# Sparse attention and a feed-forward block on one core: weight sums in halves, 2 KB store pieces, fewer zero products and a new table of steps

## The chip, the cores and the metric

The kernel runs on one core of a Trainium2 chip. The metric is the device time of one execution in microseconds, by the median of several runs. The core's engines are TensorE (PE; PEld is its weight load), VectorE (DVE), ScalarE (ACT), GpSimd (POOL) and SyncE (SP). DMAs are issued by SyncE and, for the stores of weights, by ScalarE.

## What is computed

Eight batches of attention with eight heads, 576 positions and 64 dimensions feed a feed-forward block over all 4608 tokens. Four heads see a local window of 32 positions, four see the positions of their own class modulo 32.

```python
scores = scale * np.matmul(q, k.transpose(0, 1, 3, 2))
mask_local = (rel >= 0) & (rel < stride)                      # heads 0 to 3, stride 32
mask_strided = (rel >= 0) & (pos[None, :] % stride == pos[:, None] % stride)   # heads 4 to 7
attn = np.exp(scores - scores.max(-1, keepdims=True))         # masked scores
attn = attn / (attn.sum(-1, keepdims=True) + 1e-09)
x = np.matmul(attn, v).transpose(0, 2, 1, 3).reshape(B * S, H * D)   # 4608 x 512
h = x @ w_in                                                  # 512 x 2048
g = np.where(h >= 1, h, np.where(h <= -1, 0.0, (h + 1) ** 2 / 4))
return g @ w_out                                              # 2048 x 512
```

## The kernel before

A product of float32 matrices is made of three products of 128x512 on TensorE: each operand is split into a rounded high part and a remainder. The 4608 tokens go in nine chunks of 512. The first three chunks are made directly: up(c, f) multiplies chunk c with the f-th of 16 hidden blocks, the gate g follows on ScalarE and VectorE, and for chunk 0 `down` adds the block's share of the output. The other tokens are four groups (s = 0 to 3) made by a Strassen scheme with seven products where the direct one has eight. For s = 0 only the second half of it, `down_block`, is needed; s = 1 to 3 have an `up_block` ahead of it.

The scheme needs sums of blocks of the weights. They are made once, while chunks 1 and 2 run. For pair (i, j), `whole_blocks` adds two parts of the weights (step C on GpSimd, Y on VectorE), `combine` adds on (N on GpSimd, O on VectorE), `round_sums` (R) and `rest_of_sums` (D) split the result, and `ship_sums` (S) stores it to DRAM as ks; `ship` (K) stores plain weights as kq. Later `fetch_w` loads them on SyncE's queue, 256 KB at a time, into a ring of seven buffers wr. Load n + 7 is issued when TensorE is done with n.

Attention goes in units u = 0 to 3 of each batch b (tiles named with `_b_u`). Its steps are: load qk (Q), scores on TensorE (s, tile sc), mask (m), maximum and subtraction (x, a or b, tiles pr and st), exponential (e), sum (q), reciprocal and normalisation (p, k, w, r; VectorE or GpSimd), transpose (t), a store to DRAM and a gather back as pT (j, J, on SyncE), load v (F), and value products on TensorE (v, tile xp) with copies to the next chunks' x (h, l).

All these side steps stand in AGENDA, a table of numbers. A row begins with a time t in units of six 128x512 products (1.36 us); t = 0 is up(1, 0), t = 68 the start of the first down block. A step is put into every engine's program when the loop over products comes to its time, so the table alone sets the order on each engine and in SyncE's queue. A step with zeros (`zero`) issues products of zeros in the first batch, which keep TensorE going while it has no operands.

Of the kernel before, what the change touches and what calls it, by code (L numbers as in the profile page):

```python
# [1326 lines left out]
```

## Time and profile before

| | |
|---|---|
| median of three runs | 806.49 us (804.26 to 806.54) |
| the profiled execution | 806.21 us, its span 804.4 us |
| TensorE busy | 793.8 us, 99% of the span |
| VectorE busy | 620.6 us, 77% |
| ScalarE busy | 505.2 us, 63% |
| GpSimd busy | 258.2 us, 32% |
| DMA | 209.78 MB, 261 GB/s in the mean |

All times of rows are in us from the start of the span of that one execution. A row's line number (L499) is the line of the kernel before; the changed kernel's lines are 7 or 8 higher.

### The profile page before, as it was taken

Reading aid. Unit: us, or ns where it says so; the run is one execution under the profiler, and the core shown is the slowest. Engines: PE = TensorE matmul, PEld = TensorE weight load, DVE = VectorE, ACT = ScalarE, POOL = GpSimd, SP = SyncE. Lnnn points to the kernel's source line nnn. Section 1 sums busy time; section 2 is a strip of 40 time slices with the busy share of each in tenths; the row PEclk is TensorE's granted clock in tenths of the full one; section 3 lists DMA queues with packets and bytes.
Section 4 is the critical chain, followed back from the end, with each engine's and each line's share of the span. In section 5 each row is a group of like instructions: output and inputs, shape, how many; then the busy total and the mean of one; then the engine's idle time right before and its main releaser. Section 6 shows DMA issues by size and latency. Waiting matters only on the chain.

```text
span 804.4 us, 17840 instructions
## 1 busy us (share of the span) xinstructions
PE 793.8 (99%) x6921; PEld 648.5 (81%) x6921; DVE 620.6 (77%) x882; ACT 505.2 (63%) x857; POOL 258.2 (32%) x202
## 2 busy tenths in 40 slices
PE   8999999999999999999999999999999999999998
PEld 6778888788888877878888888888888888888886
DVE  5899879999898999978679787575777764566673
ACT  5899764566774555677764455778554667775442
POOL 5366335796674320022141102132434001224000
PEclk9999999999999999999999999999999999999999
DMA  9948878799899899898889778777777676666765
GB/s 348 407 187 273 319 271 324 254 290 307 282 322 319 292 295 352 272 295 275 256 247 292 239 222 266 261 233 211 223 248 239 210 238 198 192 194 189 217 200 170
DMA packets 107699, 209.78 MB, mean 261 GB/s; under 512 B 17760, under 2 KB 33376, under 8 KB 105568
## 3 DMA queue, kind: packets, MB, share of 16 engines
q1 hardware_dynamic: 100560, 179.15, 69.8%
q10 hardware_dynamic: 7056, 29.49, 9.5%
q8 instruction: 55, 0.90, 0.4%
q14 instruction: 28, 0.23, 0.1%
HBM read 161.94 MB, written 46.66 MB: 259 GB/s over the span
## 4 chain that ended last, share of the span: by engine, by line
PE 91%; DVE 5%; ACT 1%; DMA 1%; issue 1%; POOL 1%; SPq 0%; POOLq 0%; DVEq 0%
PE yo L1135 22%; PE y L1040 16%; PE h L887 13%; PE zo L1135 10%; PE z L1040 8%; PE xo L1135 5%; PE o L947 4%; PE x L1040 4%; PE xp L779 3%; PE sc L592 3%; DMA qk<-in_qk_s 1%; PE tp L719 1%; DVE st L512 1%; DVE pr L682 1%; DVE st L678 0%
## 5 line engine op out<-in xcount | busy, mean ns | idle before, releaser
L1135 PE MATMUL yo<-hl,wr 128*128 128x512 f32 x768 | 177.6, 390 | 0.0
L1135 PEld LDWEIGHTS yo<-hl,wr 128*128 128x128 f32 x768 | 143.6, 188 | 30.9 <-DVE hl L997 0.9
L1040 PE MATMUL y<-x,wr 128*128 128x512 f32 x576 | 139.9, 389 | 0.0
L1040 PEld LDWEIGHTS y<-x,wr 128*128 128x128 f32 x576 | 108.0, 188 | 22.5
L887 PE MATMUL h<-xq_a,w 128*128 128x512 f32 x384 | 123.5, 395 | 1.9 <-DVE g L897 1.9
L1096 POOL TENSOR_TENSOR ga<-gb,ga 128x1024 f32<-128x1024 f32 x17 | 44.1, 2598 | 235.9 <-DVE ga L897 175.6
L997 DVE TENSOR_TENSOR hl<-ga,hl 128x1024 fp32r<-128x1024 f32 x48 | 63.5, 1338 | 37.0 <-ACT hl L996 36.9
L1135 PE MATMUL zo<-hl,wr 128*128 128x512 f32 x384 | 89.5, 391 | 0.0
L887 PEld LDWEIGHTS h<-xq_a,w 128*128 128x128 f32 x384 | 72.0, 188 | 18.6 <-DVE g L897 2.8
L1135 PEld LDWEIGHTS zo<-hl,wr 128*128 128x128 f32 x384 | 71.5, 188 | 15.9 <-DVE hl L997 0.6
L996 ACT CAST hl<-ga 128x1024 fp32r<-128x1024 f32 x48 | 50.0, 1052 | 51.1 <-PE yo L1135 16.3
L887 PE MATMUL h<-xq_b,w 128*128 128x512 f32 x192 | 73.6, 391 | 0.1
L1040 PE MATMUL z<-x,wr 128*128 128x512 f32 x288 | 73.5, 391 | 0.0
L1040 PEld LDWEIGHTS z<-x,wr 128*128 128x128 f32 x288 | 53.7, 188 | 11.4 <-DVE ga L1022 0.2
L894 ACT ACTIVATE tmp<-tmp 128x512 f32<-128x512 f32 x96 | 60.8, 634 | 3.0
L997 DVE TENSOR_TENSOR hl<-gb,hl 128x1024 fp32r<-128x1024 f32 x36 | 48.7, 1366 | 14.4 <-ACT hl L996 14.3
L996 ACT CAST hl<-gb 128x1024 fp32r<-128x1024 f32 x36 | 37.7, 1056 | 31.3 <-PE zo L1135 15.3
L504 POOL TENSOR_TENSOR st<-st 128x256 f32<-128x256 f32 x48 | 50.5, 1054 | 14.2 <-DVE st L705 6.6
L897 DVE SCALAR_TENSOR_TENSOR ga<-ga,tmp 128x512 f32<-128x512 f32 x48 | 33.0, 688 | 28.3 <-ACT tmp L894 28.0
L891 ACT ACTIVATE u<-h,half 128x512 f32<-128x512 f32 x48 | 32.8, 684 | 31.4 <-PE h L887 23.9
L469 POOL TENSOR_TENSOR raw<-raw 128x512 uint32<-128x512 uint32 (+1 forms) x34 | 35.6, 1057 | 42.3 <-DVE raw L465 16.6
L682 POOL TENSOR_TENSOR pr<-pr,st 128x384 f32<-128x384 f32 (+3 forms) x17 | 25.6, 1508 | 67.8 <-DVE st L678 67.8
(124 smaller groups left out, 1413.1 us busy)
## 6 DMA issues: line engine op xcount, KB each, us to landing
wr<-ks SPq DMA_DIRECT2D x224, 256.0 KB, 4.0
wr<-kq SPq DMA_DIRECT2D x168, 256.0 KB, 3.4
ks<-st ACTq DMA_DIRECT2D x16, 1024.0 KB, 6.8
raw<-in_w SPq DMA_DIRECT2D x30, 512.0 KB, 9.6
qk<-in_qk_s SPq DMA_DIRECT2D x16, 604.0 KB, 6.4
qk<-in_qk_l SPq DMA_DIRECT2D x16, 576.0 KB, 6.4
kq<-w ACTq DMA_DIRECT2D x16, 512.0 KB, 3.6
v<-in_v_l SPq DMA_DIRECT2D x21, 384.0 KB, 5.2
```

Of the source, the lines that this page charges most:

```text
L469: nc.gpsimd.tensor_tensor(out=raw[:, :, 1], in0=raw[:, :, 1], in1=raw[:, :, 0], op=ALU.add)
L504: eng.tensor_tensor(out=st[:, to, 1], in0=st[:, x, 1], in1=st[:, y, 1], op=op)
L682: eng.tensor_tensor(out=pr, in0=pr, in1=st[:, 0].unsqueeze(2).broadcast_to(list(pr.shape)), op=ALU.add)
L887: nc.tensor.matmul(o_ps[c, f], weight(f, 0, h)[:, x, e:e + P], xq[c][y][:, cc], start=first and n == 0, stop=last and n == len(todo) - 1)
L891: nc.scalar.activation(u, h, AF.Relu, bias=half, scale=0.5)
L894: nc.scalar.activation(u, u, AF.Square)
L897: nc.vector.scalar_tensor_tensor(out=to, in0=h, scalar=1.0, in1=u, op0=ALU.max, op1=ALU.min)
L996: nc.scalar.copy(t[:, 0], src)
L997: nc.vector.tensor_tensor(out=t[:, 1], in0=src, in1=t[:, 0].bitcast(F32), op=ALU.subtract)
L1040: nc.tensor.matmul(to, w_[:, a, c * P:(c + 1) * P], xc[m][:, b, c], start=m in (1, 2, 5) and c + q == 0, stop=c == 1 and q == 2, skip_grou ...
L1096: eng.tensor_tensor(out=to, in0=x, in1=y, op=op)
L1135: nc.tensor.matmul(to, w_[jj][:, a, d * P:(d + 1) * P], t[:, b, jj], start=m in (1, 2, 5) and k + jj + q == 0, stop=k == NP // 2 - 1 and j ...
```

## The change

A weight sum on GpSimd becomes two instructions of 128x512 where it was one of 128x1024; on VectorE it stays one. The DRAM tiles of weights and sums get the block index in front, so that a store writes pieces of 2 KB (kq 4 and 2 KB, ks 8 KB before) and a ring load reads one run of 256 KB. The products of zeros are as wide as their tile, up to 384 columns, and 24 where they were 37. AGENDA is new behind batch 0 (for batch 0 only the counts of zeros change), and MORE, the set of products that use two further PSUM banks, goes with it. Of the table the diff shows the rows that place batch 5's first qk loads (5Q0) and its unit 1 (5s1).

```diff
 AGENDA = """
--66.69 0Zs0:17 0o0 0s0 0o1 0i0 0X0 0s1 0i1 0S0 0o3 0g1 0x1 0s2 0Zv0:3 0Zf0:3 0m2 0e0 0a1 A0.0 0s3 0i3 0e1 0x2 0q0
+-66.69 0Zs0:10 0o0 0s0 0o1 0i0 0X0 0s1 0i1 0S0 0o3 0g1 0x1 0s2 0Zv0:2 0Zf0:2 0m2 0e0 0a1 A0.0 0s3 0i3 0e1 0x2 0q0
...
-69 G0p33 5Q0
...
-103 G0s52 5Q2 O07 G0s53 5s1 D06 5m1 R07 D07 5x1 5a1
...
+71 4e3 G0s13 R05 G0t60 D05 5Q0 G0s20
...
+77 4t2 4j2 5s1 5m1 5x1
...
+97 5Q2 G0s73 5m0 5x0 Y07
...
-    kept = [[(dram.tile([P, 3, 2, HF], F32, tag=f"kq{i}{j}", name=f"kq_{i}_{j}"),
-              dram.tile([P, 4, 2, HF], F32, tag=f"ks{i}{j}", name=f"ks_{i}_{j}")) for j in range(NP)] for i in range(2)]
+    kept = [[(dram.tile([3, P, 2, HF], F32, tag=f"kq{i}{j}", name=f"kq_{i}_{j}"),
+              dram.tile([4, P, 2, HF], F32, tag=f"ks{i}{j}", name=f"ks_{i}_{j}")) for j in range(NP)] for i in range(2)]
...
-        nc.scalar.dma_start(kept[i][j][0][:, :2], t[:, :2])
-        nc.scalar.dma_start(kept[i][j][0][:, 2], t[:, 3])
+        nc.scalar.dma_start(kept[i][j][0][:2].rearrange("a p x e -> p a x e"), t[:, :2])
+        nc.scalar.dma_start(kept[i][j][0][2], t[:, 3])
...
-        eng.tensor_tensor(out=st[:, :, 1], in0=t[:, :, 0], in1=t[:, :, 1], op=ALU.add)
+        for at in (slice(0, 2), slice(2, 4)) if eng is nc.gpsimd else (slice(0, 4),):
+            eng.tensor_tensor(out=st[:, at, 1], in0=t[:, at, 0], in1=t[:, at, 1], op=ALU.add)
...
-        nc.scalar.dma_start(kept[i][j][1], sums.pop((i, j)))
+        nc.scalar.dma_start(kept[i][j][1].rearrange("a p x e -> p a x e"), sums.pop((i, j)))
...
-            N = min(t.shape[1], 256)
+            N = t.shape[1]
...
-            nc.sync.dma_start(ring[n].bitcast(F32), kept[i][j][which][:, at])
+            nc.sync.dma_start(ring[n].bitcast(F32), kept[i][j][which][at])
...
-    MORE = set("2s2 2v0 2v1 3s0 3s2 3v1 4s0 4s1 4v0 5s0 5s2 5v1 5v2 6s3 7s0 7s1 7v0 7v1".split())
+    MORE = set("2s2 2v0 2v1 3s1 3s2 3v0 4s0 4s2 4v0 4v1 5s0 5s2 5v1 5v2 6s3 7s0 7s1 7s2 7v0 7v2".split())
```

On VectorE, in the stage of up(1, f), after the second transpose of batch 2's unit 1, the order before is this (pr_2_3 and pr_2_2 are units 3 and 2 of batch 2, g_1_0 the gate's result, st_1_3 a weight sum):

```order
L743 STREAM_TRANSPOSE t_2_1_1_2112<-pr_2_1_2039 128x3x2x32
L678 TENSOR_REDUCE st_2_3_2102<-pr_2_3_2101 128x10
L682 TENSOR_TENSOR pr_2_3_2101<-pr_2_3_2101,st_2_3_2102 128x10x54
L652 TENSOR_TENSOR pr_2_2_2135<-sc_2_2_0_2073,m_str_95 128x6x54
L652 TENSOR_TENSOR pr_2_2_2135<-sc_2_2_1_2074,m_str_95 128x6x54
L897 SCALAR_TENSOR_TENSOR g_1_0_1979<-h_1_2_2021,u_1_2_2117 128x512
L678 TENSOR_REDUCE st_2_2_2136<-pr_2_2_2135 128x12
L693 TENSOR_REDUCE st_2_3_2102<-pr_2_3_2101 128x10
```

and now, from the same transpose on:

```order
L751 STREAM_TRANSPOSE t_2_1_1_2073<-pr_2_1_1940 128x3x2x32
L660 TENSOR_TENSOR pr_2_3_2100<-sc_2_3_0_2078,m_str_95 128x4x54
L660 TENSOR_TENSOR pr_2_3_2100<-sc_2_3_1_2079,m_str_95 128x4x54
L660 TENSOR_TENSOR pr_2_3_2100<-sc_2_3_0_2078,m_str_95 64x2x54
L660 TENSOR_TENSOR pr_2_3_2100<-sc_2_3_1_2079,m_str_95 64x2x54
L905 SCALAR_TENSOR_TENSOR g_1_0_1974<-h_1_2_2021,u_1_2_2112 128x512
L686 TENSOR_REDUCE st_2_3_2101<-pr_2_3_2100 128x10
L690 TENSOR_TENSOR pr_2_3_2100<-pr_2_3_2100,st_2_3_2101 128x10x54
L660 TENSOR_TENSOR pr_2_2_2138<-sc_2_2_0_2042,m_str_95 128x6x54
L660 TENSOR_TENSOR pr_2_2_2138<-sc_2_2_1_2043,m_str_95 128x6x54
L507 TENSOR_TENSOR st_1_3_2143<-w_1_3_1067 128x4x256
L686 TENSOR_REDUCE st_2_2_2139<-pr_2_2_2138 128x12
```

The gate of h_1_2 (line L897, now L905) has moved ahead of the reduction and the subtraction (L678 and L682, now L686 and L690) of unit 3 and the masks of unit 2. The subtraction of unit 2, which GpSimd had, is on VectorE now, and so is the sum of block (1, 3).

In SyncE's queue, early in the ring loads for the first down block, batch 5's first two qk loads stand before behind ring load 8:

```order
L971 DMA wr_6_3565<-kq_1_6_181 128x512
L971 DMA wr_7_3581<-kq_1_7_183 128x512
L971 DMA wr_8_3583<-kq_1_0_169 128x512
L525 DMA qk_5_0_3586<-in_qk_l 128x1152
L525 DMA qk_5_1_3588<-in_qk_l 128x1152
L971 DMA wr_9_3602<-kq_1_1_171 128x512
L971 DMA wr_10_3604<-kq_1_2_173 128x512
```

and now behind ring load 10:

```order
L979 DMA wr_6_3557<-kq_1_6_181 128x512
L979 DMA wr_7_3573<-kq_1_7_183 128x512
L979 DMA wr_8_3575<-kq_1_0_169 128x512
L979 DMA wr_9_3607<-kq_1_1_171 128x512
L979 DMA wr_10_3609<-kq_1_2_173 128x512
L533 DMA qk_5_0_3618<-in_qk_l 128x1152
L533 DMA qk_5_1_3620<-in_qk_l 128x1152
L979 DMA wr_11_3637<-kq_1_3_175 128x512
L979 DMA wr_12_3639<-kq_1_4_177 128x512
```

On TensorE, the scores of batch 5's unit 1 begin before behind the products of ring loads 34 and 35:

```order
L1135 MATMUL zo_0_0_4052<-hl_0_17_4074,wr_34_3998 128x512 x3
L1135 MATMUL zo_0_0_4052<-hl_0_17_4074,wr_35_4018 128x512 x3
L1135 MATMUL zo_0_1_4053<-hl_0_17_4074,wr_34_3998 128x512 x3
L1135 MATMUL zo_0_1_4053<-hl_0_17_4074,wr_35_4018 128x512 x3
L592 MATMUL sc_5_1_0_4107<-qk_5_0_3586 32x64
```

and now behind those of ring loads 8 and 9:

```order
L1143 MATMUL xo_0_0_3674<-hl_0_4_3622,wr_8_3575 128x512 x3
L1143 MATMUL xo_0_0_3674<-hl_0_4_3622,wr_9_3607 128x512 x3
L1143 MATMUL xo_0_1_3675<-hl_0_4_3622,wr_8_3575 128x512 x3
L1143 MATMUL xo_0_1_3675<-hl_0_4_3622,wr_9_3607 128x512 x3
L600 MATMUL sc_5_1_0_3699<-qk_5_0_3618 32x64
```

They stood behind the 18th pair of ring loads of the first down block and now stand behind the fifth, 13 pairs of twelve products or 156 products of 128x512 earlier, while the two loads that they read are issued two ring loads later.

## Rows read from the trace of the kernel before

**Rows 1.** The head of the page, and the row of busy time that has TensorE: busy us (share of the span), instructions.

```profile
span 804.4 us, 17840 instructions
...
PE 793.8 (99%) x6921; PEld 648.5 (81%) x6921; DVE 620.6 (77%) x882; ACT 505.2 (63%) x857; POOL 258.2 (32%) x202
```

**Rows 2.** What TensorE waited for, in the whole span, by the line that waits and what it waits for: us in total, times, longest.

```profile
PE h L887 <- DVE g L897: 1.9, 2, 1.3
PE sc L577 <- DVE zeros L378: 1.0, 1, 1.0
PE sc L592 <- DMA qk<-in_qk_s: 0.6, 1, 0.6
PE o L947 <- DVE w L482: 0.5, 2, 0.4
```

**Rows 3.** TensorE's timeline in the stage up(1,f): start us, us, engine, line, operation, out<-in, count [idle before, released by].

```profile
142.84 0.39 PE L887 MATMUL h<-xq_b,w 128*128 128x512 f32 x1
143.07 0.39 PE L887 MATMUL h<-xq_a,w 128*128 128x512 f32 x1
144.80 0.50 PE L887 MATMUL h<-xq_a,w 128*128 128x512 f32 x1 [1.34 <-DVE g L897]
...
151.91 0.39 PE L887 MATMUL h<-xq_a,w 128*128 128x512 f32 x1
152.88 0.50 PE L887 MATMUL h<-xq_a,w 128*128 128x512 f32 x1 [0.58 <-DVE g L897]
```

**Rows 4.** VectorE's timeline in the same stage and shortly before it, columns as in rows 3.

```profile
130.89 1.04 DVE L743 STREAM_TRANSPOSE t<-pr 128x384 f32<-128x384 f32 x2
...
140.64 2.57 DVE L682 TENSOR_TENSOR pr<-pr,st 128x540 f32<-128x540 f32 x1
143.25 0.90 DVE L652 TENSOR_TENSOR pr<-sc,m_str 128x324 f32<-128x324 f32 x2
144.06 0.68 DVE L897 SCALAR_TENSOR_TENSOR g<-h,u 128x512 f32<-128x512 f32 x1
...
151.21 1.04 DVE L743 STREAM_TRANSPOSE t<-pr 128x384 f32<-128x384 f32 x2 [1.40 <-POOL pr L706]
```

**Rows 5.** GpSimd's timeline in the same stage, columns as in rows 3.

```profile
140.23 2.40 POOL L499 TENSOR_TENSOR st<-w 128x1024 f32<-128x1024 f32 x1
...
148.70 2.48 POOL L706 TENSOR_TENSOR pr<-pr,st 128x540 f32<-128x540 f32 x2 [1.86 <-DVE st L705]
```

**Rows 6.** Groups of instructions by line, the first two of GpSimd by shape, the third of VectorE over four shapes: out<-in, count | busy us, mean ns of one | idle before.

```profile
L469 POOL TENSOR_TENSOR raw<-raw 128x512 uint32<-128x512 uint32 x30 | 33.0, 1110 | 37.0 <-DVE raw L465 16.6 <-ACT raw L461 8.4 <-ACT w L478 4.8
L499 POOL TENSOR_TENSOR st<-w 128x1024 f32<-128x1024 f32 x9 | 24.2, 2690 | 4.1 <-PE h L887 2.1 <-DMA ks<-st 2.0
...
L682 DVE TENSOR_TENSOR pr<-pr,st 128x540 f32<-128x540 f32 (+3 forms) x14 | 13.2, 940 | 0.3
```

**Rows 7.** Batch 5's second pair of qk loads: SyncE's queue (timeline), the time from issue to landing of the loads issued in 288 to 302 us, and TensorE's timeline where they are used.

```profile
289.69 0.86 SPq L525 DMA_DIRECT2D qk<-in_qk_s  x2
...
DMA to landing us min/median/max: 7.8/9.2/10.5
...
300.69 0.57 PE L592 MATMUL sc<-qk 64*64 64x54 f32 x24 [0.57 <-DMA qk<-in_qk_s]
```

**Rows 8.** TensorE's timeline at the first value products of batch 5.

```profile
343.83 0.30 PE L779 MATMUL xp<-pT,v 64*64 64x32 f32 x4
344.35 1.59 PE L779 MATMUL xp<-pT,v 64*64 64x32 f32 x92 [0.21 <-DMA pT<-there]
```

**Rows 9.** Batch 5's first pair of qk loads: SyncE's queue, the landing of the two qk loads issued in 238 to 272 us, and a stretch of the windows view (busy us of each engine and instructions, then granted clock of TensorE, DMA share, GB/s).

```profile
242.35 3.72 SPq L971 DMA_DIRECT2D wr<-kq  x4
...
DMA to landing us min/median/max: 4.8/5.8/6.8
...
245.00:250.00 5.00, 5.00 (x24) 4.14 (x23) 3.97 (x5) 2.58 (x3) 4.76 (x4) 1.00 0.97 364
```

**Rows 10.** Batch 4's first v loads, by tile (min/median/max ns of an issue, first and last start; landing), and TensorE's timeline where they are used and where the first down block begins.

```profile
L538 SPq DMA_DIRECT2D v<-in_v_l x2: 334/1106/1877, 223.2 to 223.9; - x2
...
DMA to landing us min/median/max: 8.1/8.7/9.3
...
235.53 1.70 PE L779 MATMUL xp<-pT,v 64*64 64x32 f32 x95
237.27 3.01 PE L1135 MATMUL yo<-hl,wr 128*128 128x512 f32 x12
```

**Rows 11.** Batch 2's first value products on TensorE's timeline, and the landing of the four gathers that they read.

```profile
147.75 1.60 PE L779 MATMUL xp<-pT,v 64*64 64x32 f32 x96
...
DMA to landing us min/median/max: 2.2/3.6/4.6
```

**Rows 12.** The products of zeros of the first batch's scores, by line (min/median/max ns, first and last start), and the stretch of low clock in the windows view.

```profile
L577 PE MATMUL sc<-zeros x17: 396/421/421, 1.0 to 4.4; 128*128 128x256 bf16 x17
...
20.50:23.80 3.30, 3.16 (x31) 2.72 (x29) 3.07 (x8) 2.13 (x9) 1.47 (x2) 0.53 1.04 416
```

**Rows 13.** DMA issues by kind, of the whole span: count, KB each, median us from issue to landing.

```profile
wr<-ks SPq DMA_DIRECT2D x224, 256.0 KB, 4.0
wr<-kq SPq DMA_DIRECT2D x168, 256.0 KB, 3.4
ks<-st ACTq DMA_DIRECT2D x16, 1024.0 KB, 6.8
```

More of the change, by code (lines that the diff above doesn't have):

```diff
@@ new lines @@
+22.5 N13 R13 2r3 2j2 3b0
+23.95 S14 2t3
+24.5 Y16
+25.45 3e0 3q0 3p0
+26.5 3m1 C17 D13 3r0 S13 N17 D12
+27.45 3Q2
+28.5 3s2 2J2
+29.95 2v2 2h2 3x1 3a1 D15 S15 3t0
+31.45 2j3 2J3 2l2 K02 3m2 3x2
+31.95 3b2 3e1 3q1 3k1
+32.5 2F4 3j0
+33.95 3w1 3s3 3t1 2V1 2h3 2h1 3j1 2l3 N16
+34.5 C00
+35.95 3e2 3m3 3x3 3a3
+36.5 3q2 3p2 S12 3r2
+39.45 3F1
+41.45 Y02
+41.95 3t2
+43.45 3e3 4Q0 R16 D16 S16
+43.95 3q3 C01 Y03 R17 D17 N02 4s0 4m0 K07 S17
+44.5 4x0 R02
+46.5 4b0
+47.45 D02 4s1 3J0 3J1 N00 3j2 3F0 3v0 R00 D00 4e0 N03
@@ new lines @@
+124.5 X1.5
+125.5 5s3 5s2 5m2 X1.4 5x2
+126.5 5b2
+127.5 5q1
+129.5 5e2 5q2 5J0
+133.5 5k1 5k2 5w2 5t2 6Q0 5m3
+134.5 5j2
+135.5 5x3
+136.5 5r1 5b3
+137.5 5t1
+138.5 5j1 5e3 5q3 5k3 5r3 5v0 5h0 5F3
+146.5 5J2 6s0 6m0 6x0 G1s11
+150.5 6s1 5t3 5v2 5h2 5j3 6Q2 6a0 6e0
+151.5 6m1 6q0
+153.5 6k0 6w0 6t0
+154.5 5J1
+159.5 5F2
+160.5 5F4 6x1
+162.5 5J3 6a1 6e1 G1t61
+163.5 G1s10 G1p60
+168.5 6q1
+170.5 6j0 6k1 6r1 6F1 6s2 6m2 6x2 5V1 5h3 6J0
+171.5 5h1
+172.5 6b2
+174.5 6t1
+179.5 G1s12 G1t62 6F0
+181 6j1 G1s13 6e2 6q2
@@ new lines @@
+183 G1s20 6k2
+185 G1s21
+187 G1s22 G1r11 G1t42
+189 7Q0 G1s23 G1r10 6r2 6F3 6s3 6v0 6h0 G1p63
+191 6t2 6j2 G1t41
+193 G1s60 G1s61
+195 G1s62 G1r20 6m3 6x3
+197 G1p43 6J2 G1s63
+199 G1s70 6a3 6e3 G1p50
+201 G1s71 6J1
+203 G1r61 G1r60 6q3 6p3 6w3 6t3 7s0 6v2 G1s72
+205 6j3 G1s73
+207 G1s50
+209 6h2 G1r21 6F2 G1p51 G1s51
+211 G1p52 G1s52
+213 G1t53 G1s53 7m0
+215 G1s30
+217 G1t40 7x0
+219 6J3 G1r50 G1s31 G1r51 6F4 G1s32
+223 G1r00 7a0 7e0 7q0 G1s33 7k0
+225 G1s41 7r0 6V1 G1s40 7s1
+227 G1r30 G1r01 6h3
@@ new lines @@
+229 G1r31 7m1 7x1
+231 G1s42 7b1 7Q2
+233 G1s43 X2.1 X2.-7 X2.-6 X2.7 X2.-5 X2.2
+235 G1r40 X2.6 7t0 G1r41 X2.5 7j0
+237.5 X2.3
+238.5 7s2
+239.5 X2.-4 7e1 7q1 7k1 7w1 7t1
+241.5 X2.4
+242.5 7m2
+243.5 7j1
+244.5 6h1
+251.5 7J0
+258.5 G2s11
+262.5 G2s10
+264.5 7x2 7b2
+267.5 G2p61
+268.5 7e2 7q2 7F0 7k2 7r2 7J1
+278.5 G2t60
+281.5 7t2 7j2 7F1
+291.5 7v0 G2s12 7s3 7m3 7h0 X3.1
+293 G2s13 7x3 7a3
+295 G2s20
+297 7e3 7q3
+299 G2s21 G2p62 G2s22 7F3 G2p63
+301 G2r11 G2s23 G2p43
+303 7F4 G2s60
+305 G2s61
@@ L256 @@
+307 G2r10 G2s62
+309 G2s63 7k3 7w3 7t3 G2t42 7J2
+311 G2s70 7j3
+313 G2s71
+315 G2r60 G2t51 G2t50 G2r61
+317 G2s73 7v2
+319 G2s72 7F2
+321 G2p41
+323 7h2 G2r21 G2p52 G2s50
+325 G2r20 G2t53 7J3 G2s51
+327 G2s52 G2s53
+329 G2s31
+331 G2r50 G2s30 G2r51 G2r01 7V1
+335 G2s32 G2r00 7h3 X3.2 G2s33
+337 7h1 X3.-7 G2p40 G2s40 G2s41
+339 G2r30 G2s42
+341 G2s43
+343 X3.-6 X3.6 G2r31
+345 X3.7 X3.-5
+347 G2r40 X3.5
+348.5 X3.3
+349.5 G2r41
+352.5 X3.-4 X3.4
+365.5 G3s10
+370.5 G3s11 G3p60
+396.5 G3p61
 403.5 G3s12
```

376 lines of the change are left out of this document (129 added, 247 removed).

## The prediction

> **What bounds the kernel now.** I read the page's busy shares first [rows 1]: TensorE is busy for 793.8 of 804.4 us. It is the bound almost everywhere, so a change can win only what TensorE still waits for, or what it need not compute. The program of matmuls is the same before and after, apart from the zero products, and their order among the attention products leaves the same number of changes between product kinds. So I went to the list of TensorE's waits [rows 2]. It holds 1.9 us for VectorE's gate result g, 1.0 us of start-up, 0.6 us for a qk load, 0.5 us for weights; the others are start-up or smaller. A little over 3 us of that lies behind batch 0, which is where the new layout acts. That is the ceiling of any gain, and it is close to what a measurement here can tell from no change: 0.3% of 806.49 is 2.4 us, so 804.1 to 808.9 counts as no change.
>
> Where these waits lie, by the timelines. In up(1,·) the product at 143.07 is followed by one at 144.80; the distance before it is 0.23 us (0.227 with one more digit), so 1.50 us is lost. After the one at 151.91 comes 152.88: 0.74 lost [rows 3]. Both end with g. VectorE's own rows say why [rows 4]: `pr<-pr,st` at 140.64 took 2.57 us, and g stood behind it and two masks until 144.06. The mean over that line's 14 instructions is 0.94 [rows 6]; here it ran beside a GpSimd weight sum of 128x1024 from 140.23 to 142.63 [rows 5], and it ended 0.6 us after that sum. The second time VectorE sat 1.40 us idle before a transpose whose input GpSimd's normalisation (two, 148.70 to 151.18) made late, with g queued behind it.
>
> **The change, part by part.** The profiled execution took 806.21 us, 1.8 more than its span and 0.28 below the median of 806.49. The sum below is made against 806.21 and then raised by 0.28.
>
> *Wait for g.* In the new order VectorE does g(1,2) ahead of the reduction and `pr<-pr,st` of batch 2's unit 3, not behind them, and normalises unit 2 itself, so no transpose there waits for GpSimd. The sum that lay beside it now belongs to block (1,2) and comes in halves. I count both as gone: −1.50 −0.74 = −2.24.
>
> *Halves.* A sum of 128x1024 takes 2.69 us on GpSimd in the mean, a 128x512 of another type 1.11 [rows 6]. Two halves thus cost between 2×1.11 = 2.2 and 2×2.69/2 + one start each; I take 2×1.3 = 2.6, no change within 0.2 us for each of eight sums (nine before; one moves to VectorE). GpSimd is far from full, and the sums' products are stored tens of microseconds before they are loaded, so this costs TensorE nothing; if that cover were gone it would be 8×0.2 = 1.6. What it can give is that VectorE, where blocked, is blocked for 1.3 and not 2.4 us. The Trainium skill ("SBUF — State Buffer", section "SBUF: two separate sides") says that a VectorE instruction with two SBUF inputs and a GpSimd one that reads SBUF exclude each other for a whole instruction, whoever starts first. The 2.57 us row above agrees: it ended just after the 2.40 us sum. By that rule the halved sum alone, in the old order, would give back about 1.1 of the 1.50 us; in the new order nothing more.
>
> *Loads of qk.* A qk pair of batch 5 is issued at 289.69, lands after 7.8 and 10.5 us, and its products wait 0.57 us at 300.69 [rows 7]. In the new order the same pair stands six units (8.2 us) earlier relative to its ring load, and its products run later. Gone: −0.6.
>
> *Gathered probabilities.* At 343.83 four value products start, then 0.21 us idle, and 96 end at 345.94, 2.11 us where a run without a wait takes 1.60 [rows 8, 11]. The new order gives that gather three units (4.1 us) more. Gone: −0.5.
>
> *Zeros.* 37 products of 256 columns become 24 of up to 384: 9472 columns become at most 9216. The first 17 fill the time until the first qk lands and cost 0.42 us each [rows 12]; the last of them end with the load, so I take −0.1, between −0.4 and 0.
>
> *Pieces of 2 KB.* The stores of the sums and weights write 2 KB pieces; each later 256 KB load then reads one contiguous block. Loads from tiles whose pieces lie 6 KB apart land in 3.4 us, 8 KB apart in 4.0 [rows 13]; no row shows 0 apart, so a load gains between 0 and 0.6 us or more, and the list has no wait of TensorE for a ring load: 0. The stores of the sums land in 6.8 us. Their new price lies between 0 and, if a packet cost as much at a quarter of the size, four times that; it is hidden unless the DMA engines are full where something is awaited. They are nearly full around 240 us (below). The Trainium skill ("DMA: Bandwidth & Descriptors", section "Why small descriptors are slow (HBM only)") gives a fixed overhead of about 3 cycles for each packet, with 32 bytes a cycle. By that estimate 2 KB pieces take 67 cycles for 64 of payload, against 259 for 256 at 8 KB: 3.5% longer stores, 0.24 us on 6.8. No run shown here has such stores. By the rule, term (a) below would be 1.1 and the sum −1.4; by the rows alone it stays as it is.
>
> *What the new order makes tight.* Three places.
> (a) The products of batch 5's unit 1 stand at product 828 of the program (ten units into the first down block), where before they stood 156 products later. Their loads are issued behind ring load 10, on SyncE's queue. The four ring loads 9 to 12 issue between 242.35 and 246.07 [rows 9], so the pair goes out at about 243.7 and 244.2. Landing here takes 4.8 to 6.8 us: 248.5 and 251.0. The first down block begins at 237.27 [rows 10], so unit ten begins at 237.27 + 60×0.227 = 250.9, and its second half at 251.3. Slack 0.3, at a DMA share of 0.97 [rows 9] and with the stores of two sums in the same stretch. At the 7.8 and 10.5 us of the other qk pair it would be 3.4 us late. Bounds 0 to 3.4; nearer the row of this place: I take 0.9.
> (b) The v loads of batch 4 wait for buffers that value products of batch 3 leave; these move 12 products (2.72 us) later. Before, they issue from 223.2 on, land after 8.1 and 9.3 us, and are used from 235.53: slack 2.3 [rows 10]. Bounds 0 to 2; I take 0.4.
> (c) Batch 2's first value products, at 147.75 before, move 12 products ahead (to about 145.0, or 143.5 without the wait for g), while the transpose they need, at 130.89 to 131.93 [rows 4], has some 2.8 us more VectorE work ahead of it: 134.7. A store of about 2 us, four gathers issued some 0.5 us apart that land in 2.2 to 4.6 us [rows 11], and the last is there between 142 and 144. Bounds 0 to 1.3; I take 0.5.
>
> In the weight stage (24 to 60 us) the order of conversions on VectorE and ScalarE changes too. Two waits for weights lie there, 0.5 us together [rows 2]. By counting the VectorE work ahead of each conversion, five get 1.1 to 3.7 us later and their slack is up to 2.4; two on ScalarE get 2 us earlier. I take 0 between −0.6 and +1.5.
>
> Sum: −2.24 −0.6 −0.5 −0.1 + 0.9 + 0.4 + 0.5 = −1.6, so 806.21 − 1.6 = 804.6, and with 0.28: **804.9 us**.
>
> **Rivals.**
> *The full gain.* All removable waits go and none of (a) to (c) shows: −3.4, perhaps −0.5 more where the weights come early: 803.1 to 802.6, in the middle 802.8 us. For it: each new slack is positive or nearly so at the median landing. Against it: three places with little slack at once.
> *Slower: loads late at the first down block.* The DMA engines are at 0.97 there, and stores in four times as many packets join. If landings there are as at 289.69 (10.5 us), (a) costs 3.4 and (b) 1.2 + 2.72 − 2.3 = 1.6; the ring load queued behind the late pair on SyncE costs up to 2 more, and hl's products with it. 7 − 3.4 = +3.6: 810 us. It decides from 5.8 us of new waits, where the gain of 3.4 is used up and 2.4 more. Against it: this pair's like landed in 4.8 to 6.8 us at the same place.
> *Nothing moves.* The waits for g go, and as much comes back at (a) to (c) and in the weight stage: 806.5 ± 1.
> *The clock.* From 20.5 to 23.8 us the granted clock was 0.53 [rows 12]. Fewer zeros early may place or lengthen such a stretch; as long again costs 3.3×0.47 = 1.6 us: 806.5.
>
> **How the numbers follow.** Forecast as summed 0.43 (own range 802.8 to 807), full gain 0.24, late loads 0.15, nothing moves 0.13, clock 0.05. Faster by over 0.3% needs less than 804.1: nearly all of the full gain and a third of the forecast's case, 0.39. Slower than 808.9: the late loads and a little of the rest, 0.17. The rest, 0.44, is no change. The range from 801.8 to 809.2 takes in the bounds of (a) to (c) one at a time and leaves out most of the late loads.
>
> **What would show it.** Right: no wait for g among TensorE's waits between 140 and 155 us, none for qk near 300 us, and TensorE's idle time in the rows of batch 5's unit 1, batch 4's and batch 2's first value products adding to 1 to 3 us. VectorE's instructions beside a weight sum blocked for 1.3 us at most. Wrong: a wait for qk or v of several us between 235 and 255 us, ring loads landing later than 4.4 us there, more or longer waits for weights before 60 us, or a longer stretch of low clock.

## The result: 0.5% slower, and where the time went

Over ten executions each, the kernel before has a median of 806.33 us and the changed one of 809.44 us (807.68 to 813.97). The ratio is 1.0054, with a 95% interval of 1.0036 to 1.0072: 3.1 us slower by the medians and about 4 by the ratio, where 1.6 us faster was forecast and 809.2 was the end of the range. The profiled execution took 813.72 us and is among the longest of its ten; two further profiles of the same kernel have spans of 810.9 and 809.5 us (812.85 and 811.39 us). All three are longer than the median, so they show more loss than the median has. What all three show belongs, as far as three can tell, to the kernel; what only one shows does not.

The head of the page of the changed kernel, and the pieces that answer to [rows 1] and [rows 13]:

```profile
span 811.8 us, 17797 instructions
...
PE 796.0 (98%) x6908; PEld 648.0 (80%) x6908; DVE 622.7 (77%) x879; ACT 505.6 (62%) x852; POOL 263.6 (32%) x218
...
wr<-ks SPq DMA_DIRECT2D x224, 256.0 KB, 3.5
wr<-kq SPq DMA_DIRECT2D x168, 256.0 KB, 3.3
ks<-st ACTq DMA_DIRECT2D x16, 1024.0 KB, 6.6
...
kq<-w ACTq DMA_DIRECT2D x16, 512.0 KB, 6.3
```

TensorE's busy time has grown by 2.2 us and its span by 7.4: the time is in waits, and in a stretch of low clock (a granted clock at the lower of its two levels, 1.2 and not 2.4 GHz). TensorE's timeline of the changed kernel, only the instructions behind 24 us with a wait ahead of them; the bracket has the idle time and what ended it:

```profile
81.61 0.47 PE L895 MATMUL h<-xq_a,w 128*128 128x512 f32 x1 [0.56 <-DVE gl L923]
125.62 0.30 PE L600 MATMUL sc<-qk 64*32 64x64 f32 x2 [1.29 <-DVE pr L660]
126.09 0.75 PE L600 MATMUL sc<-qk 64*32 64x64 f32 x46 [0.17 <-DVE pr L660]
144.79 1.99 PE L787 MATMUL xp<-pT,v 64*64 64x32 f32 x96 [0.96 <-DVE pr L660]
161.84 0.50 PE L895 MATMUL h<-xq_a,w 128*128 128x512 f32 x1 [1.97 <-DVE g L905]
184.44 1.46 PE L787 MATMUL xp<-pT,v 54*64 54x64 f32 x40 [2.19 <-issue]
259.20 0.46 PE L600 MATMUL sc<-qk 64*32 64x64 f32 x24 [0.19 <-DMA qk<-in_qk_l]
304.03 5.78 PE L1143 MATMUL zo<-hl,wr 128*128 128x512 f32 x24 [0.73 <-ACT kept L1124]
320.57 7.78 PE L1143 MATMUL yo<-hl,wr 128*128 128x512 f32 x33 [0.27 <-DMA wr<-kq]
```

These add to 8.3 us; the same list of the kernel before adds to 3.2 (1.34 + 0.58 for g, 0.57 for qk, 0.21 for the gather, 0.53 for weights). So 5.1 of the 7.4 us are waits, and four places between 125 and 185 us alone hold 6.6 us of them. Of the three waits that the change was to remove [rows 3, 7, 8] none is left. Nearly all of the loss lies ahead of the first down block, which began at 237.27 before [rows 10]:

```profile
244.56 11.34 PE L1143 MATMUL yo<-hl,wr 128*128 128x512 f32 x48
```

Directly behind the wait at 184 us the clock is low. The windows view (busy us by engine, then granted clock, DMA share, GB/s):

```profile
176.00:180.00 4.00, 4.00 (x19) 3.31 (x18) 4.00 (x8) 1.92 (x6) 3.84 (x5) 1.00 0.87 269
180.00:184.00 4.00, 2.25 (x92) 1.75 (x90) 3.86 (x8) 2.47 (x5) 3.45 (x5) 1.00 1.03 355
184.00:188.00 4.00, 3.56 (x45) 3.08 (x46) 1.86 (x8) 1.52 (x10) 0.00 (x0) 0.50 0.60 188
188.00:192.00 4.00, 4.00 (x13) 3.11 (x13) 2.41 (x7) 0.78 (x2) 0.77 (x1) 0.65 0.92 320
```

The granted clock is at its lower level, 1.2 GHz, until about 191 us. In the second profile it is low until about 188 us. In the third, with a wait of 2.72 us at the same place, it stays at 2.4 GHz:

```profile
184.00:188.00 4.00, 3.93 (x53) 3.38 (x54) 2.05 (x7) 1.54 (x10) 0.00 (x0) 1.00 0.56 139
```

From the end of this wait to the 41st product of 128x512 behind it the first profile takes 12.9 us, the second 11.6 and the third 10.1: the low clock cost 2.8 and 1.5 us. In the first profile 5.1 us of waits and 2.8 us of low clock make 7.9. Against that the changed kernel reaches up(1, 0) 1.3 us sooner: at 23.86 us, and the kernel before at 25.16, behind its own stretch of low clock [rows 12]. That leaves 6.6 of the 7.4 us; some 0.8 us are in no wait of the list.

### The profile page after: what moved, and what is told of

It reads as the page before. It is cut to its first block, busy times and chain, and to the rows that moved or that the text cites. A ratio compares the mean times of both kernels' runs of the same rounds, so it can differ in the third digit from the quotient of the medians.

```text
span 811.8 us, 17797 instructions
## 1 busy us (share of the span) xinstructions
PE 796.0 (98%) x6908; PEld 648.0 (80%) x6908; DVE 622.7 (77%) x879; ACT 505.6 (62%) x852; POOL 263.6 (32%) x218
## 4 chain that ended last, share of the span: by engine, by line
PE 80%; DVE 7%; DMA 6%; ACT 3%; issue 2%; ACTq 1%; POOL 0%; SPq 0%; DVEq 0%; POOLq 0%
PE yo L1143 19%; PE y L1048 16%; PE h L895 10%; PE zo L1143 9%; PE z L1048 8%; PE xo L1143 5%; PE x L1048 4%; PE xp L787 3%; PE sc L600 2%; PE o L955 2%; DMA there<-t 2%; DMA raw<-in_w 1%; DMA qk<-in_qk_l 1%; DVE hl L1005 1%; DMA wr<-kq 1%
## 5 line engine op out<-in xcount | busy, mean ns | idle before, releaser
L895 PE MATMUL h<-xq_a,w 128*128 128x512 f32 x384 | 125.2, 399 | 2.7 <-DVE g L905 2.0
L1005 DVE TENSOR_TENSOR hl<-ga,hl 128x1024 fp32r<-128x1024 f32 x48 | 72.3, 1525 | 30.9 <-ACT hl L1004 30.9
L905 DVE SCALAR_TENSOR_TENSOR ga<-ga,tmp 128x512 f32<-128x512 f32 x48 | 34.4, 719 | 22.6 <-ACT tmp L902 22.5
L1004 ACT CAST hl<-g 128x1024 fp32r<-128x1024 f32 x28 | 29.3, 1052 | 30.0 <-PE yo L1143 14.3
```

Source lines behind the costliest of these rows:

```text
L895: nc.tensor.matmul(o_ps[c, f], weight(f, 0, h)[:, x, e:e + P], xq[c][y][:, cc], start=first and n == 0, stop=last and n == len(todo) - 1)
L905: nc.vector.scalar_tensor_tensor(out=to, in0=h, scalar=1.0, in1=u, op0=ALU.max, op1=ALU.min)
L1004: nc.scalar.copy(t[:, 0], src)
L1005: nc.vector.tensor_tensor(out=t[:, 1], in0=src, in1=t[:, 0].bitcast(F32), op=ALU.subtract)
```

## Four waits, read from the queues

*Scores at 125 us.* VectorE's mask (L660) at 125.03 frees their bank. Ahead of it on VectorE stands the remainder of the first weight sum, which waited for ScalarE. ScalarE's timeline:

```profile
118.76 1.53 ACTq L498 DMA_DIRECT2D kq<-w  x1
120.33 1.20 ACTq L497 DMA_DIRECT2D kq<-w  x1
121.57 1.01 ACTq L498 DMA_DIRECT2D kq<-w  x1
122.67 1.05 ACT L516 CAST st<-st 128x1024 fp32r<-128x1024 f32 x1 [2.97 <-POOL st L512]
```

The rounding (L516) could not start before the two stores of weights ahead of it had been issued. An issue of such a store takes 0.34 to 0.37 us at the least; here three took 3.7 us. They started back to back and were long in themselves. What made them long was not shown; the DMAs that last had their completion semaphores (see the next place) had landed at least 3.5 us before, so that is not it.

*Gate at 161 us.* Again stores stand ahead on ScalarE, with the gate's u behind them. Here the issues are short, but start late:

```profile
156.89 0.40 ACTq L497 DMA_DIRECT2D kq<-w  x1
159.28 0.34 ACTq L498 DMA_DIRECT2D kq<-w  x1
159.72 0.69 ACT L899 ACTIVATE u<-h,half 128x512 f32<-128x512 f32 x1 [5.92 <-DMA kq<-w]
```

What holds these two is in the program. Every DMA, whichever queue issues it, takes one of eight completion semaphores in turn (in the trace each of the eight has 86 to 89 DMAs), and waits until the DMA that had it before has landed. These are instructions of the changed kernel with their waits, first on SyncE, then on ScalarE:

```
L772 DMA pT_2_1_2107<-there_2_1_2075 32x4x96 [waits DMAHW7_49,DMAHW3_49]
L772 DMA pT_2_1_2107<-there_2_1_2075 32x4x96 [waits DMAHW4_49]
...
L497 DMA kq_1_5_179<-w_1_5_1340 128x2x512 [waits DMAHW3_49]
L498 DMA kq_1_5_179<-w_1_5_1340 128x512 [waits DMAHW4_49]
```

The two stores have the semaphores of the first two gathers of batch 2's unit 1. In the trace these landed at 156.9 and 159.3 us: the stores' issue times. The gathers were late because the stores to DRAM that they read were issued at 146.3 us, in one bunch with the two qk loads of batch 3 and a store of weights:

```profile
142.62 1.83 SPq L942 DMA_DIRECT2D out<-ob  x4
144.54 1.69 SPq L533 DMA_DIRECT2D qk<-in_qk_l  x2
146.32 2.10 SPq L761 DMA_DIRECT2D there<-t  x2
...
155.11 1.76 SPq L772 DMA_DIRECT2D pT<-there  x4
```

The two stores took 8.7 and 7.4 us to land, at a DMA share of 1.01 and 1.00 from 144 to 152 us. The landing (min/median/max) of these stores and the gathers that read them, in the changed kernel between 134 and 160 us:

```profile
DMA to landing us min/median/max: 1.8/3.6/8.7
```

and in the kernel before between 130 and 145 us:

```profile
DMA to landing us min/median/max: 1.9/2.1/4.6
```

So TensorE waited for VectorE, that for ScalarE, that for a store's turn, that for a gather on another queue, and that for slow stores in a bunch of about 2 MB (two loads of 576 KB, stores of 512 and 256). The links up to the gather are read from the queues; that the bunch made the stores slow is argued from the DMA share alone.

*Value products at 144 and 184 us.* Those at 144 us wait for two things that come almost together. One is their gather, as term (c) said: the last part of it landed at 144.56 (143.92 and 143.88 in the other two profiles). The other is the first of the two masks of unit 2 on VectorE, which frees their bank: the scores of unit 2 (2s2) and these products (2v0) both stand in MORE. It ended at 144.68 (144.20 and 144.17), 0.07 us ahead of the products' first weight load in all three profiles. So the mask ended the wait, as the bracket says, 0.1 to 0.3 us behind the gather. At 184 us, unit 3's products need a v load and a gather. Both need a buffer that unit 2's products leave at 175 us, four product units earlier; the old table had nine. SyncE's queue has the gathers first, then the load, which landed after 6.5 us, at 184.4:

```profile
167.39 2.05 SPq L761 DMA_DIRECT2D there<-t  x2
175.12 2.73 SPq L772 DMA_DIRECT2D pT<-there  x4
177.89 0.47 SPq L546 DMA_DIRECT2D v<-in_v_s  x1
```

## Which part of the change: the table and the pieces

**e1: everything but the table.** The kernel before, with the diff of this document except AGENDA and MORE (the zeros' counts in the first rows of AGENDA are the new ones).

> The kernel before with everything of the change but the table: halves, 2 KB pieces and the wider zeros, under the old AGENDA and MORE. Theory order (the new table makes the waits): within 0.3% of before, 805 to 808 us, and the two waits for g at 144 and 152 us of before stay or shrink to about 1 us together. Theory pieces (stores in 2 KB pieces land later and hold up what is behind them): slower by 2 to 4 us, the kq stores landing in about 6 us and not 3.6.

805.48 us against 805.58, ratio 0.9995 (0.9978 to 1.0012). Halves, pieces and zeros together do nothing under the old table that this interval can tell. In its profile VectorE's subtraction beside the halved sum took 1.47 us and not 2.57, the 1.1 us that the prediction had estimated, and TensorE's wait for g behind it 0.87 and not 1.34; the second wait for g stayed (0.59). Stores of weights land in 3.8 us: their 6.3 us in the changed kernel are the new order's, not the pieces'. The theory of the pieces falls.

**e2: the table alone.** The kernel before with the new AGENDA and MORE.

> The kernel before with the new AGENDA and MORE alone; sums whole, stores in 8 KB and 4 KB pieces, zeros as before. Theory order: 3 to 4 us slower than before, with TensorE waits at batch 2's scores (near 125 us), for g (near 162 us) and for v (near 184 us) as in the changed kernel. Theory pieces: 1 to 2 us faster than before, kq landing in about 3.6 us and those waits under 1 us together.

818.54 us, ratio 1.0166 (1.0137 to 1.0194). The sign is as the theory of the order has it, the size is three to four times as large: some 13 us. (AGENDA and MORE were not tried apart.) Of the waits that were expected near 125, 162 and 184 us its profile has 0.17 us at 125, none near 162 (but 1.08 at 174), and 1.05 at 182. **e3: the changed kernel without the pieces** (DRAM tiles, stores and loads of before) says the same:

> The changed kernel with the DRAM tiles, stores and loads of before (8 KB and 4 KB pieces). Theory order: as the changed kernel, 808 to 811 us. Theory pieces: 803 to 806 us, waits for g near 162 us and v near 184 us gone.

819.68 us, ratio 1.0178 (1.0145 to 1.0211). So under the new table the pieces are worth 9 to 10 us, and under the old one nothing that can be told. The first down block begins at 240.57 us in e2, and in e3 at:

```profile
241.33 11.22 PE L1143 MATMUL yo<-hl,wr 128*128 128x512 f32 x48
```

That is 3 to 4 us later than before and earlier than in the changed kernel; the other 9 us of both lie behind it. TensorE's timeline of e3 shows where, and the windows what follows:

```profile
259.36 9.42 PE L1143 MATMUL xo<-hl,wr 128*128 128x512 f32 x33 [1.91 <-DMA wr<-kq]
300.36 10.50 PE L1143 MATMUL zo<-hl,wr 128*128 128x512 f32 x45 [1.34 <-DMA wr<-ks]
321.62 12.11 PE L1143 MATMUL yo<-hl,wr 128*128 128x512 f32 x45 [2.98 <-DMA wr<-kq]
```

```profile
260.00:264.00 4.00, 4.00 (x12) 3.16 (x11) 3.31 (x4) 1.04 (x1) 0.00 (x0) 0.57 0.75 269
322.00:326.00 4.00, 4.00 (x12) 3.17 (x11) 0.05 (x1) 0.43 (x1) 0.00 (x0) 0.58 0.62 222
```

The first of the three is the ring load that stands behind batch 5's moved qk pair on SyncE: the forecast's own rival of late loads, at the place and near the 2 us that it named. The new table leaves the ring loads little slack there. Pieces take 0.5 us off a load from ks (4.0 to 3.5 in the median, [rows 13] and above). The waits for ring loads are 6.2 us in e3, with low clock behind two of them, against 0.3, 1.6 and 1.7 in the three profiles of the changed kernel.

The landing of the ring loads issued between 240 and 262 us, in e3:

```profile
DMA to landing us min/median/max: 3.1/5.7/10.4
```

and in the changed kernel:

```profile
DMA to landing us min/median/max: 3.1/6.5/8.7
```

There it is not the median that fell, but the longest. The third profile of the changed kernel lets one load be compared: the ring load behind the qk pair goes out at 249.18 us in e3 and at 249.19 there. Its landing, in e3 and then in that profile:

```profile
DMA to landing us min/median/max: 10.1/10.1/10.1
DMA to landing us min/median/max: 8.2/8.2/8.2
```

TensorE waits 1.91 us for the one and 0.17 for the other. Both sides of the pieces, stores in 2 KB and loads from one run, change in e3 together; which of them does it was not tried.

**e4 and e15: the changed kernel again.**

> The changed kernel once more, unaltered, for a second profile. Both theories: 808 to 814 us. If the stretch of low clock behind the wait near 184 us is part of every execution, it is here too; if the clock falls only in the executions in which that wait is long, the span here is shorter by about 2 to 4 us wherever the stretch is missing.

> The changed kernel, a third profile. If its waits are fixed by the order alone, the four waits (scores near 125 us, value products near 144 us, g near 161 us, value products near 184 us) are within 0.5 us of the other two profiles. If they hang on how loads happen to land, one of them or more differs by over 1 us.

e4: 810.27 us in the median of four, span of the profile 810.9. e15: 811.39 us, span 809.5. The waits near 125, 144, 161 and 184 us are 1.06, 0.88, 1.96, 2.57 us in e4 and 1.05, 0.82, 1.54, 2.72 in e15: all four in each, within 0.6 us of the first profile. They belong to this order with these parts: e2 and e3 have the same order, and there the first is 0.2 and 1.0 us, the third none and 0.75. Low clock follows the last in two of three.

## Mending one place at a time

Each of these is the changed kernel with rows of AGENDA altered.

**e5: the v load of unit 3 earlier.**

```diff
-29.95 2v2 2h2 3x1 3a1 D15 S15 3t0
+29.95 2v2 2F4 2h2 3x1 3a1 D15 S15 3t0
-32.5 2F4 3j0
+32.5 3j0
```

> The changed kernel with one step moved: batch 2's last v load (2F4) stands on SyncE's queue ahead of the stores and gathers of unit 3, not behind them. Theory v load (the wait near 184 us is for this load, and the low clock behind it is its consequence): that wait (2.2 to 2.6 us) and the low clock from 185 to 190 us (about 2 us) go, so 3.5 to 4.5 us faster than the changed kernel, 805 to 806 us. Theory that TensorE waits there for its gathered probabilities: no change of the wait, 809 to 810 us.

815.26 us, ratio 1.0114 (1.0093 to 1.0136): 5 us worse. The load now stands in SyncE's queue ahead of unit 3's stores and waits there for its buffer until 174.6 us; the stores go out at 175.0, where they went at 167.4. VectorE's transposes need the stores' buffers, and its timeline shows the price:

```profile
179.90 1.04 DVE L751 STREAM_TRANSPOSE t<-pr 128x384 f32<-128x384 f32 x2 [3.46 <-DMA there<-t]
```

TensorE then waited 1.85 us for copies behind it and 1.05 us for the gather. **e9** puts the load between the stores and the gathers.

```diff
-31.45 2j3 2J3 2l2 K02 3m2 3x2
+31.45 2j3 2F4 2J3 2l2 K02 3m2 3x2
-32.5 2F4 3j0
+32.5 3j0
```

> As e5, but the v load of batch 2's unit 3 stands between that unit's stores and its gathers, so the stores, and the transposes on VectorE that need their buffers, no longer wait behind it. Theory v load: the wait near 184 us falls from 2.2 to 2.6 us to under 1 us and the low clock behind it goes, no wait on xq_b takes its place: 3 to 4 us faster than the changed kernel, 806 us. If the gathers behind the load are then what is awaited: 1 us faster at most.

810.65 us, ratio 1.0058 (1.0043 to 1.0073): no gain. The wait is as long, but names its other cause:

```profile
183.65 0.80 PE L787 MATMUL xp<-pT,v 54*64 54x64 f32 x36 [2.23 <-DMA pT<-there]
```

The v load alone was not the cause. **e12** moves unit 2's products, which free both buffers, two steps ahead, on top of e9:

```diff
-28.5 3s2 2J2
+28.5 3s2 2J2 2v2
-29.95 2v2 2h2 3x1 3a1 D15 S15 3t0
+29.95 2h2 3x1 3a1 D15 S15 3t0
```

> The changed kernel with batch 2's unit 2 value products 1.5 product units (2 us) earlier, directly behind their gather's issue, and the v load of unit 3 between that unit's stores and gathers. Theory buffers (both loads of unit 3 wait for unit 2's products): the wait near 184 us falls by about 2 us to 0.5 us or less and no low clock follows: 3 to 4 us faster than the changed kernel, 805 to 806.5 us. If the gather is late for the load of the DMA engines alone: it stays near 2 us, 809 to 810 us.

The wait near 184 us is gone, and no low clock follows: the theory of the buffers holds for it. But the median is 809.76 us, ratio 1.0037 (1.0015 to 1.0059). Instead TensorE waits 1.48 us for g at 174.8 us, and 1.66 at 144 where it was 0.96. On ScalarE a store of a sum was held, by a qk load this time:

```profile
168.38 0.38 ACTq L523 DMA_DIRECT2D ks<-st  x1
168.81 0.85 ACT L697 ACTIVATE pr<-pr 128x768 f32<-128x768 f32 x1 [3.69 <-DMA qk<-in_qk_s]
```

**e6: the rounding ahead of two stores.**

```diff
-0.95 N10 K05 K06 R10 D10 S10 2Q0 2s0
+0.95 N10 R10 D10 K05 K06 S10 2Q0 2s0
```

> The changed kernel with the rounding and remainder of the first weight sum (R10, D10) ahead of two stores of weights (K05, K06) on ScalarE, not behind them. Theory held ScalarE (ScalarE sits at the store's issue, waiting for a semaphore of an earlier DMA, and with it the remainder and the mask on VectorE that free the bank of the scores): the wait of 0.9 to 1.5 us near 125 us goes, 1 us faster than the changed kernel, 808 to 809 us. If VectorE is late for another reason: the wait stays.

The wait near 125 us is gone: the rounding starts at 120.9 us, ahead of the stores, where it started at 122.7 behind them.

```profile
120.91 1.05 ACT L516 CAST st<-st 128x1024 fp32r<-128x1024 f32 x1 [1.97 <-POOL st L512]
```

So the stores on ScalarE were its cause, by issues that were long and not by a semaphore, as had been expected. The median is 810.81 us, ratio 1.0056 (1.0035 to 1.0076): nothing gained, with 1.6 us at the value products near 143 us and low clock behind them in its profile. The wait near 161 us is gone from it too, though its store was not moved.

**e7: the store K15 later.**

```diff
-17.45 N14 R14 K15 D14
+17.45 N14 R14 D14
-22.5 N13 R13 2r3 2j2 3b0
+22.5 N13 R13 2r3 2j2 3b0 K15
```

> The changed kernel with one store of weights (K15) issued on ScalarE some five products' units later, so that it no longer stands ahead of the gate of up(1,6). Theory held ScalarE: the wait of 2.0 us for g near 161 us goes, 2 us faster than the changed kernel, about 807.5 us. If g is late because VectorE or GpSimd is full there: it stays, 809 to 810 us.

816.16 us, ratio 1.0126 (1.0109 to 1.0143). The wait near 161 us goes, and 5.03 us come at 172.86. I had overlooked that a weight sum on VectorE (Y16) waits for that store's landing, with g behind it:

```profile
170.98 1.23 DVE L507 TENSOR_TENSOR st<-w 128x1024 f32<-128x1024 f32 x1 [5.41 <-DMA kq<-w]
172.12 0.68 DVE L905 SCALAR_TENSOR_TENSOR g<-h,u 128x512 f32<-128x512 f32 x1
```

**e10** moves it only behind the gate.

```diff
-17.45 N14 R14 K15 D14
+17.45 N14 R14 D14
+17.95 K15
```

> As e7, but the store of weights K15 stands only one gate later on ScalarE, directly behind the gate of up(1,6) that waited for it, so that the weight sum on VectorE which needs its landing (Y16) is not put off. Theory held ScalarE: the 2.0 us wait for g near 161 us falls to under 0.5 us and no 5 us wait near 172 us comes: 1.5 to 2 us faster than the changed kernel, 807.5 us. If g(1,6) is not late because of that store: no change, 809.5 us.

810.31 us, ratio 1.0056 (1.0041 to 1.0071). The wait near 161 us is gone from its profile, 1.48 us for g at 174.16 are there instead: as e12. The store was what the gate waited for, as the first theory says, and moving it gave nothing, as the second one forecast.

**e8, e11, e13 and e14: several at once.** e8 is e5 to e7 together with 2v0 one row later (14.5); e11 is e6, e9, e10 and that; e13 is e11 on top of e12; e14 is e13 without the move of e10.

> The changed kernel with the three moves of e5 to e7 together and batch 2's first value products (2v0) one product unit later. If the four waits are independent: 7 to 8 us faster than the changed kernel, about 801.5 to 803 us, and 3 to 4 us faster than before. If they replace one another (the same late DMAs show up at the next place): 804 to 808 us.

> The changed kernel with the moves of e6, e9 and e10 and batch 2's first value products one product unit later. If the four places are the loss and do not replace one another: waits of about 1 us left between 100 and 240 us, 802 to 804 us, faster than before by 2 to 4 us. If the late DMAs of this stage show up at the next place: 805 to 810 us.

> e12 with the moves of e6 (first rounding ahead of two stores), e10 (store behind the gate) and batch 2's first value products one product unit later. If the places are the whole loss: 802 to 804 us, 2 to 4 us faster than before. If they replace one another: 806 to 809 us.

> e13 without the move of e10. Theory held ScalarE for the wait near 161 us: 1 to 2 us slower than e13, the wait for g near 161 us back. If that store only moves the wait to later gates: the same as e13 within 1 us.

e8: 819.86 us, with 4.52 us at 170.6 (the sum that waits for the store) and 3.80 at 186.4 (the transposes of e5). e11: 809.25 us, ratio 1.0038 (1.0021 to 1.0054), with 3.50 us at 183 for the gather and low clock behind it in its profile. e13: 809.03 us, ratio 1.0036 (1.0018 to 1.0054). e14: 809.82 us, ratio 1.0042 (1.0020 to 1.0063), within 1 us of e13 and without a wait near 161 us: moving the store of e10 makes no difference there. A second profile of e13 was taken because the first has no wait of a microsecond behind 24 us and is yet the kernel's fastest execution of ten:

> The kernel of e13, a second profile. If other waits take the place of the mended ones in the slower executions, TensorE's waits between 100 and 345 us add to 4 to 8 us here, at other places than before the moves. If the loss of its median lies elsewhere (a longer start, low clock), they add to under 4 us again.

Waits of TensorE behind 24 us, added up from each profile's timeline. Each ratio is against executions of the kernel before that were taken with that kernel, whose medians lie between 805.58 and 806.33 us:

| kernel | median us | ratio to before | waits us | low clock behind a wait |
|---|---|---|---|---|
| before, two profiles | 806.33 | 1 | 3.2, 2.8 | no |
| changed, three profiles | 809.44 | 1.0054 | 8.3, 8.6, 8.7 | yes, yes, no |
| e1 all but the table | 805.48 | 0.9995 | 4.7 | yes |
| e2 table alone | 818.54 | 1.0166 | 11.8 | yes |
| e3 changed, no pieces | 819.68 | 1.0178 | 12.5 | yes, twice |
| e13, two profiles | 809.03 | 1.0036 | 4.9, 5.1 | no, no |
| e14 as e13, store not moved | 809.82 | 1.0042 | 4.8 | no |
| e18 (below) | 804.97 | 0.9986 | 1.7 | no |

e13's two profiled executions took 807.55 and 808.73 us, with 1.6 and 1.9 us more of waits than the first profile before, at other places than the mended ones (gather at 171, copies at 184, g at 189 and 238 us): the second has 4.6 us between 100 and 345 us, just inside the 4 to 8 of its first theory. Some 0.3 us more of an execution than before lies outside the span. Its other executions reach 812.84. Two of them took 811.6 us at a mean granted clock of 1.00, so it was not low clock that made these long; what they wait for was not seen. That the mended places do not sum to the loss is shown; where the last 1 to 2 us of e13's median go is open. e14's profiled execution took 812.64 us for another reason: low clock from 17 to 31 us, ahead of and into up(1, 0), which begins at 28.07.

**e17: the kernel before again.**

> The kernel before, a second profile. If the old table's slack absorbs the spread of the landings, TensorE's waits behind 24 us are within 1 us of the first profile's 3.2 us, and at the same places.

805.93 us; waits of 2.8 us, g at the same two places with 1.34 and 0.54 us. The qk wait near 300 us is not there; ring loads have 0.50 and 0.24 us instead.

**e18: the waits for g removed in the old table.**

```diff
-10.5 2x3 2b3 2m2
+11.01 2x3 2b3 2m2
-14.5 2a2 2e2 2p3 2r3 K07 2q2 2p2 2v0 2r2 2t2 2F4 2j2
+14.5 2a2 2e2 2p3 2r3 K07 2q2 2p2 2v0 2r2
+15.01 2t2 2F4 2j2
```

> The kernel before, with two pieces of its table put behind a gate instead of ahead of it: the maximum and subtraction of batch 2's unit 3 with the masks of unit 2 behind the gate of up(1,2), and the transpose, v load and store of unit 2 behind the gate of up(1,4). If the waits for g are worth what the prediction counted: 2.2 us faster than before, about 804 us, no wait for g between 140 and 155 us. If a later wait fills the gap: 805.5 to 806.5 us, with the wait at another place in the profile.

804.97 us against 805.93, ratio 0.9986 (0.9971 to 1.0001). Both waits are gone, and one of 1.28 us came at 161.85:

```profile
161.85 0.51 PE L888 MATMUL h<-xq_a,w 128*128 128x512 f32 x1 [1.28 <-DVE g L898]
```

By the medians 1.0 of the 2.24 us stayed; the interval takes in anything from 2.3 us faster to no change. Of all kernels tried it has the lowest median.

## The prediction, step by step

- *What bounds the kernel.* Right in the main: its work is unchanged and the loss is in TensorE's waits, with 1.5 to 2.8 us of low clock behind one of them in two of three profiles.
- *Wait for g, loads of qk, gathered probabilities* (−3.3 together). All three places are free of waits in the changed kernel. But the waits for qk and for the gather, 1.1 of the 3.3 us, stood in one execution: the second profile of the kernel before (e17) has neither, nor have e1 and e18 with its table. And the wait for g, removed alone, brings 1 us by the medians and not 2.24 (e18, within its interval), with g late again 10 us on.
- *Halves.* Right as an edit without effect, as far as e1 shows it together with pieces and zeros. A half takes 1.47 us in the mean, 1.29 in the median, against the 1.3 taken. Beside the first halved sum VectorE's remainder at 130.74 took 2.08 us, where 1.2 is its time alone: blocked for 0.9, within the 1.3 forecast.
- *Pieces.* Taken as 0. No effect can be told under the old table (e1); under the new one they save 9 to 10 us (e2, e3). "The list has no wait of TensorE for a ring load: 0" was read from one execution of the old order (e17 has two such waits, 0.74 us together), where slack hid what a load costs; the new order used that slack up. This error did not make the forecast too low: without the pieces the kernel would have been 13 to 14 us slower. The Trainium skill ("DMA: Bandwidth & Descriptors", section "Why small descriptors are slow (HBM only)") has a fixed overhead for each packet, from which 0.24 us longer stores were estimated. The traces agree in direction: under the same table the stores of sums land in 7.4 us with 2 KB pieces against 6.8 (e1, before), and in 6.3 to 6.6 against 5.7 and 6.0 (three profiles of the changed kernel, e2 and e3), medians of sixteen stores.
- *Zeros.* No effect that these runs can tell.
- *What the new order makes tight.* This is the step that failed: "three places" were counted with 1.8 us, and the waits at those and at three more came to 6.4 to 6.8 us. (a) was 0 to 0.3 us in the changed kernel, 0.9 counted; without the pieces it would have been 2.4 (0.45 and 1.91 in e3), inside the bounds. (b) did not come, 0.4 counted. (c) was 0.8 to 1.0 us, 0.5 counted, and ended with a mask that the prediction did not name, just behind the gather that it did. Missing were three more places, 5.3 to 5.6 us in the three profiles: scores at 125 us and the gate at 161 us, both through stores that keep ScalarE's queue, and unit 3's loads at 184 us, through buffers that one earlier step frees. Ring loads, counted at 0, took another 0.3 to 1.7. I had followed loads from their own issue and had counted VectorE's work, but not the order of issue on ScalarE, whose busy share of 63% seemed to leave room, and not the waits of the issues themselves. That the table makes the loss is shown by e1 and e2. That these places are the whole of it is not: e13 has none of the four between 125 and 185 us and is still 3 us slower by the medians.
- *Weight stage.* Taken as 0: 0.5 to 0.6 us at 81.6 us take the place of the two waits of 0.5 us before.
- *Rivals.* The slower one had the right kind of cause, late DMAs, but at the first down block, where the loss lies 60 us and more ahead of it, and without the chain through ScalarE. It had a chance of 0.15, and slower in all 0.17.
- *The clock.* Low clock came behind a wait of TensorE and not at the start, and cost 2.8 us in the profiled execution. At the start the three profiles of the changed kernel have none, where before had 3.3 us; in e14, with the same zeros, it lasted 14 us there.
- *The signs.* Those for "right" came true or nearly so: no wait for g between 140 and 155 us, none for qk near 300, 0.9 to 1.2 us at the three places where 1 to 3 were named. They looked only where waits were expected. Two of the signs for "wrong" came too: ring loads that land in 6.5 us in the median, and the low clock.

## What to carry to other kernels

When a table of steps is laid out anew, list for every engine what stands ahead of each awaited instruction, DMA issues among it: an issue can be held by a DMA of another queue, and then the whole engine is. An edit priced at nothing under one order has to be priced again under the other. And a wait that is removed is worth its length only if what follows on the late engine has room; by the medians e18 got under half of it, and by the ratios e13, with four places mended, a third. A wait that one profile shows may be gone in the next of the same kernel: a second profile before counting on it would have taken 1.1 us out of this forecast.

## What the runs showed of the hardware

A wait of TensorE can cost twice. Behind waits of 2.19 us (changed kernel), 1.91 and 2.98 us (e3), 1.95 us (e1) and 5.03 us (e7) the granted clock was 0.50 to 0.67 in the next 4 or 5 us. Behind 2.72 us (e15), 2.23 us (e9) and 2.10 us (e2) it stayed at 1.00, and behind 0.49 and 1.12 us (e6) it was 0.56. The length of the wait alone does not decide it.

Executions of one kernel spread by more than I had expected: the 91 of the kernel before lie between 803.45 and 810.47 us, the 15 of the changed kernel between 807.68 and 813.97. A single profile can be 4 us away from the median.
